# Second products of a feed-forward turned round: weights stationary, 512 tokens moving

## The chip, the cores and the metric

The kernel runs on one core of a Trainium2 chip. The metric is the device time of one execution in microseconds. The engines are TensorE (PE; PEld is its weight load), VectorE (DVE), ScalarE (ACT), GpSimd (POOL) and SyncE (SP); the last two mainly start DMAs here.

## The reference

A block of a network: the input plus a state-space convolution plus a feed-forward, both of the layer-normed input.

```python
# x: 1 x 2048 x 576, state size 128, hidden size 4608
xn = (x - mean(x)) / sqrt(var(x) + 1e-5)
dt = exp(log_dt); A = A_re + 1j*A_im
K  = real(einsum("dn,dnl,dn->dl", C, exp(dt*A*l), dt*B))     # response, 2048 long
y  = irfft(rfft(pad(xn)) * rfft(pad(K)))[:2048] + xn * Dskip
h  = silu(xn @ w1)
out = x + y + h @ w2
```

## The kernel before

The feed-forward is the main work. The 2048 tokens are taken in two halves; the hidden size is cut into 9 chunks of 4 tiles of 128; and a block is a half, a chunk and 512 tokens (`b` 0 or 1), so there are 36 blocks. All its matmuls are made in the fast fp32r format, and each operand is split into a high and a low part (`h`, `l`), of which three products are summed.

A block has eight steps. `u0` to `u3` (`up`, L343 to L345) each make one hidden tile: 14 matmuls with 128x128 of w1 stationary and 512 tokens moving into a PSUM bank `ph`; ScalarE then makes the silu `gf` (L351) and the high part `gh` (L352), VectorE the low part `gl` (L354). `d0` to `d3` (`down`, L369) each take 128 tokens: `gh` or `gl` of 128 tokens is stationary, and 288 columns of `w2h` or `w2l` move, 12 matmuls for each half of the 576 columns, into a bank `po`. VectorE adds the bank to `acc` (L373), which begins as x. That is 96 matmuls of 288 columns in a block. `u0` of the next block stands ahead of `d0`, and `u1` to `u3` stand behind `d3`. The banks `ph` come from a round of two (`ps1`), `po` from another of two (`ps2`), and every third `po` from a fifth bank (`ps3`).

Beside this, a generator `side` makes the convolution: layernorm and transposes (`pt`, L134), the parameters, the first transform of the inputs (`spread`: `xr` loaded, split into `sp` by L166 and L167, multiplied into `pu` by L171 and L172, copied by L173, sent out as `d1u` by POOL), the response (`kgen`, 36 steps; each odd step makes `kp`, L708, 32-column tiles, then `z`, L723, two row tiles of 64, copies it to `stage` by L731 and sends it to `d1k`), the spectral stage (`pf`, L804; `pb`, L848), and the last transform (`py`, L963) with the sum. `weave` runs both generators: the side yields the share of the main steps at which it goes on. From this a scheduler that simulates the engines fixes the order of the instructions on each engine; `high_priority` and `behind` (not ahead of a named instruction) bend it. At run time each engine takes its list in order.

```python
        while at is not None and at * steps <= i + 1:
            at = next(side, None)
```

The sums of the first half go to DRAM (`dr0`), and are loaded back at the end to get their convolution added.

Of the kernel before, what the change touches and what calls it, by code (L numbers as in the profile page):

```python
# [43 lines left out]
def kernel(  # L44
# [24 lines left out]
    NCH = NFT // FT  # L69

# [15 lines left out]
    dr0 = dram.tile([8 * P, D], F32, name="dr0")  # L86
# [17 lines left out]
    accp = ctx.enter_context(tc.tile_pool(name="accp", bufs=4))  # L104
# [3 lines left out]
    ps1 = ctx.enter_context(tc.tile_pool(name="ps1", bufs=2, space=PSUM))  # L108
    ps2 = ctx.enter_context(tc.tile_pool(name="ps2", bufs=2, space=PSUM))
# [4 lines left out]
    def banks_of():  # L114

        n = 0
        while True:
            n += 1
            pool, tag = (ps3, "ps3") if ps3 and n % 3 == 0 else (ps2, "ps2")
            yield pool.tile([P, 512], F32, tag=tag, name="po")  # L120

    spare = banks_of()
# [32 lines left out]
    def spread(up):  # L155

        s1 = up.tile([P, 2, P], F32R, name="s1", bufs=1)
        nc.gpsimd.dma_start(s1, cs1)
        for j in range(NJ):
            src = up.tile([P, D], F32, tag="xr", name="xr")  # L160
            nc.sync.dma_start(src, dxn[:, j])
            for m in range(2):
                lo, hi = slice(64 * m, 64 * m + 64), slice(64 - 64 * m, 128 - 64 * m)
                u1 = up.tile([P, D], F32, tag="u1", name="u1")
                sp = up.tile([P, D], F32R, tag="sp", name="sp")
                nc.scalar.copy(sp[lo, :], src[lo, :])  # L166
                nc.vector.tensor_sub(sp[hi, :], src[lo, :], sp[lo, :])  # L167
                for h in range(2):
                    hs = slice(h * HD, (h + 1) * HD)
                    pu = pss.tile([P, 512], F32, tag="pss", name="pu")  # L170
                    nc.tensor.matmul(pu[:, :HD], s1[:, 0, :], sp[:, hs], start=True, stop=False)  # L171
                    nc.tensor.matmul(pu[:, :HD], s1[:, 1, :], sp[:, hs], start=False, stop=True)  # L172
                    nc.scalar.copy(u1[:, hs], pu[:, :HD])  # L173
                nc.gpsimd.dma_start(  # L174
                    d1u.rearrange("(p m j) d -> m j p d", m=2, j=NJ)[m, j], u1)
                yield j
# [44 lines left out]
    def phase0(p0, js, idle=None):  # L221

        xs = load_x(js[0], accp, "acc", (nc.sync, nc.scalar) if js[0] < 2 else (nc.sync,))
        acc.update(zip(js, xs))
# [42 lines left out]
    def ffn():  # L267
# [42 lines left out]
        def load_w2(half, c, t):  # L310

            first = half == 0 and c == 0
            last = half == 1 and c == NCH - 1
            r2 = (pa if first and t > 1 else yp if last and t > 1 else wp).tile([P, D], F32, tag="w2r", name="w2r", bufs=2 if t > 1 and (first or last) else 3)
            landed = nc.sync.dma_start(r2, w2v[:, c * FT + t, :]).ins
            if t < 2:
                pins["load"] = landed
            R2[half, c, t] = r2

        def split_w2(half, c, t):  # L320
            first = half == 0 and c == 0
            r2 = R2.pop((half, c, t))
            h2 = wp.tile([P, D], F32R, tag="w2h", name="w2h", bufs=FT + 1)
            l2 = wp.tile([P, D], F32R, tag="w2l", name="w2l", bufs=FT + 1)
            with behind(pins["xt_s"] if first else pins["gh"]):
                pins["w2h"] = nc.scalar.copy(h2, r2).ins
            with behind(pins["w1l"] if first else None):
# [3 lines left out]
            W2[half, c, t] = h2, l2  # L331

        def up(blk, t, a=0, e=512, after=None):
# [4 lines left out]
            pool, tag = (None, "") if e == 256 and t > 1 else (ps1, "ps1")  # L338
            ph = (pool.tile([P, 512], F32, tag=tag, name="ph") if pool else next(spare))[:, a:e]
# [16 lines left out]
        def down(blk, jj):  # L356
# [3 lines left out]
            if half == 1 and c == NCH - 1:  # L360
                if jj % 2 == 0:
                    add_conv(j, (acc[j], acc[j + 1]))
            for h in range(2):
                hs = slice(h * HD, (h + 1) * HD)
                po = next(spare)
                n = 0
                for t in range(FT):
                    for g, w in ((0, 0), (0, 1), (1, 0)):
                        pins["pe"] = nc.tensor.matmul(po[:, :HD], G[blk, t][g][:, js], W2[half, c, t][w][:, hs],  # L369
# [4 lines left out]
            if half == 0 and c == NCH - 1:  # L374
                rows = slice(j * P, (j + 1) * P)
                nc.sync.dma_start(dr0[rows, :], acc[j])
                if j % 2:
                    acc[7 + j], acc[8 + j] = load_x(7 + j, accp, "acc", (nc.sync,))
# [32 lines left out]
        yield 0  # L411

# [7 lines left out]

        for i, blk in enumerate(blocks):
            half, c, b = blk
            later = i + 1 < len(blocks)
            new = (half, c + 1) if c + 1 < NCH else (half + 1, 0)
            more = new[0] < 2
            if half == 0 and c == NCH - 1:
# [7 lines left out]
                (1, "d3"): [(split_w2, 1), (load_w2, 3), (split_w2, 2)],  # L434
                (1, "u2"): [(split_w2, 3)],
            }
            if new == (1, NCH - 1):
# [5 lines left out]
                    (1, "d3"): [(split_w2, 1), (split_w2, 2)],  # L443
                    (1, "u2"): [(split_w2, 3)],
                }
            for step in ("u0", "d0", "d1", "d2", "d3", "u1", "u2", "u3"):
                k = int(step[1])
                if step[0] == "d":
                    down(blk, k)
                    yield 3.0  # L450
                elif later:
                    up(blocks[i + 1], k)
                    yield 3.0
                for f, t in after.get((b, step), ()) if more else ():
                    f(*new, t)
                if half == 0 and c == NCH - 1:
# [25 lines left out]
    def natural(nat, par):  # L482
# [32 lines left out]
        lrT = nat.tile([P, D], F32, tag="lrT", name="lrT")  # L515
# [639 lines left out]
```

## Time and profile before

| | |
|---|---|
| median of 3 runs | 1099.55 us (1099.28 to 1099.86) |
| profiled execution | 1099.23 us, of which the span of instructions is 1097.4 |
| granted TensorE clock | 1.00 of full speed |
| busy | PE 1090.0, PEld 963.2, DVE 888.0, ACT 658.9, POOL 136.6 us |
| stages (by the side's work) | start to 40 us, inputs and response to about 650, spectral 673 to 960, last transform to the end |

Times are microseconds from the start of the span. In rows that group instructions, the number behind the bar is busy time, then the mean in ns, then the idle time of the engine before them and what ended it. Matmuls overlap in the pipeline, so the mean duration of one is longer than its share of time; the chain of waits gives the share, since it lists how much later the next piece began.

### The profile page before, as it was taken

Reading aid. Unit: us, or ns where it says so; the run is one execution under the profiler, and the core shown is the slowest. Engines: PE = TensorE matmul, PEld = TensorE weight load, DVE = VectorE, ACT = ScalarE, POOL = GpSimd, SP = SyncE. Lnnn points to the kernel's source line nnn. Section 1 sums busy time; section 2 is a strip of 40 time slices with the busy share of each in tenths; the row PEclk is TensorE's granted clock in tenths of the full one; section 3 lists DMA queues with packets and bytes.
Section 4 is the critical chain, followed back from the end, with each engine's and each line's share of the span. In section 5 each row is a group of like instructions: output and inputs, shape, how many; then the busy total and the mean of one; then the engine's idle time right before and its main releaser. Section 6 shows DMA issues by size and latency. Waiting matters only on the chain.

```text
span 1097.4 us, 23933 instructions
## 1 busy us (share of the span) xinstructions
PE 1090.0 (99%) x9807; PEld 963.2 (88%) x9807; DVE 888.0 (81%) x1431; ACT 658.9 (60%) x1030; POOL 136.6 (12%) x241
## 2 busy tenths in 40 slices
PE   9999999999999999999999999999999999999998
PEld 7989998999889898999899988888888888898886
DVE  7799899999999999989999945886777777753443
ACT  4575457666776676677766744675676656552220
POOL 1101000000000000010000024223232312000111
PEclk9999999999999999999999999999999999999999
DMA  9845522524343525264755147356555545326953
GB/s 257 219 124 156 147 62 62 121 70 112 95 99 108 108 73 126 80 138 141 201 151 120 65 95 240 120 163 179 176 184 147 159 132 175 120 95 167 240 162 88
DMA packets 174142, 150.23 MB, mean 137 GB/s; under 512 B 112288, under 2 KB 143792, under 8 KB 173904
## 3 DMA queue, kind: packets, MB, share of 16 engines
q1 hardware_dynamic: 156544, 93.77, 33.4%
q0 software_dynamic: 16736, 54.07, 15.7%
q8 instruction: 77, 1.26, 0.5%
q10 hardware_dynamic: 752, 0.85, 0.3%
q14 instruction: 33, 0.27, 0.1%
HBM read 104.13 MB, written 44.61 MB: 136 GB/s over the span
## 4 chain that ended last, share of the span: by engine, by line
PE 98%; DVE 1%; DMA 0%; issue 0%; POOL 0%; ACTq 0%; DVEq 0%; ACT 0%
PE po L369 42%; PE ph L343 36%; PE kp L708 3%; PE pf L804 3%; PE ph L345 3%; PE ph L344 3%; PE pb L848 2%; PE z L723 2%; PE pu L171 1%; PE py L963 1%; PE pu L172 1%; PE pt L134 0%; DMA acc<-in_A_u_dram 0%; DVE w1l L305 0%; DVE st L203 0%; PE ptk L502 0%
## 5 line engine op out<-in xcount | busy, mean ns | idle before, releaser
L369 PE MATMUL po<-w2h,gh 128*128 128x288 f32 x1152 | 338.4, 296 | 0.0
L369 PE MATMUL po<-w2l,gh 128*128 128x288 f32 x1152 | 337.4, 295 | 0.0
L369 PE MATMUL po<-w2h,gl 128*128 128x288 f32 x1152 | 335.9, 296 | 0.0
L369 PEld LDWEIGHTS po<-w2h,gh 128*128 128x128 f32 x1152 | 215.5, 188 | 13.6 <-issue 5.3
L369 PEld LDWEIGHTS po<-w2l,gh 128*128 128x128 f32 x1152 | 215.6, 188 | 6.9 <-issue 1.1
L369 PEld LDWEIGHTS po<-w2h,gl 128*128 128x128 f32 x1152 | 214.9, 188 | 1.6 <-issue 0.2
L373 DVE TENSOR_TENSOR acc<-po,acc 128x288 f32<-128x288 f32 x288 | 125.9, 450 | 101.5 <-PE po L369 100.2
L351 ACT ACTIVATE gf<-ph 128x512 f32<-128x512 f32 (+1 forms) x146 | 85.7, 588 | 178.9 <-PE ph L345 164.0
L343 PE MATMUL ph<-xl,w1h 128*128 128x512 f32 (+1 forms) x584 | 159.1, 387 | 0.0
L343 PE MATMUL ph<-xh,w1h 128*128 128x512 f32 (+1 forms) x584 | 158.7, 388 | 0.0
L343 PE MATMUL ph<-xh,w1l 128*128 128x512 f32 (+1 forms) x584 | 158.7, 386 | 0.0
L354 DVE TENSOR_TENSOR gl<-gf,gh 128x512 fp32r<-128x512 f32 (+1 forms) x148 | 98.1, 669 | 47.8 <-ACT gh L352 47.1
L343 PEld LDWEIGHTS ph<-xl,w1h 128*128 128x128 f32 x584 | 107.1, 188 | 21.3 <-issue 0.7
L343 PEld LDWEIGHTS ph<-xh,w1l 128*128 128x128 f32 x584 | 107.0, 188 | 20.2
L343 PEld LDWEIGHTS ph<-xh,w1h 128*128 128x128 f32 x584 | 104.0, 188 | 18.1 <-issue 0.8
L352 ACT CAST gh<-gf 128x512 fp32r<-128x512 f32 (+1 forms) x148 | 89.1, 610 | 39.3 <-PE po L369 36.5
L174 POOL DMA_DIRECT2D d1u<-u x32 | 17.4, 543 | 462.3 <-ACT u L173 460.4
L667 ACT ACTIVATE c<-th 128x1040 f32<-128x1040 f32 x36 | 38.7, 1075 | 45.9 <-DVE th L666 45.9
L665 ACT ACTIVATE c<-th,magic 128x1040 f32<-128x1040 f32 x36 | 42.1, 1168 | 26.1 <-DVE C L688 23.2
L305 DVE TENSOR_TENSOR w1l<-w1r,w1h 128x640 fp32r<-128x640 f32 x72 | 56.8, 816 | 0.1
L345 PE MATMUL ph<-x,w1l 128*128 128x512 f32 (+1 forms) x146 | 56.7, 389 | 0.0
L344 PE MATMUL ph<-x,w1h 128*128 128x512 f32 (+1 forms) x146 | 56.5, 388 | 0.0
(195 smaller groups left out, 1725.9 us busy)
## 6 DMA issues: line engine op xcount, KB each, us to landing
w2r<-in_B_w_dram SPq DMA_DIRECT2D x72, 288.0 KB, 4.3
w1r<-in_B_w_dram SPq DMA_DIRECT2D x35, 512.0 KB, 3.9
d1u<-u POOLq DMA_DIRECT2D x32, 288.0 KB, 2.9
d1k<-stage SPq DMA_DIRECT2D x36, 256.0 KB, 4.8
u<-d1u POOLq DMA_DIRECT2D x16, 576.0 KB, 5.6
kw<-d1k POOLq DMA_DIRECT2D x16, 576.0 KB, 4.7
d<-yo POOLq DMA_DIRECT2D x32, 288.0 KB, 3.0
ys<-d SPq DMA_DIRECT2D x32, 288.0 KB, 8.5
```

The source lines that it names most:

```text
L305: pins["w1l"] = nc.vector.tensor_sub(l1, src, h1).ins
L343: nc.tensor.matmul(ph, w[:, kt, :], v[:, kt, a:e], start=n + kt == 0, stop=False)
L344: nc.tensor.matmul(ph, h1[:, 4, :], x4[:, a:e], start=False, stop=False)
L345: pins["pe"] = nc.tensor.matmul(ph, l1[:, 4, :], x4[:, a:e], start=False, stop=True).ins
L351: nc.scalar.activation(gf, ph, AF.Silu)
L352: pins["gh"] = nc.scalar.copy(gh, gf).ins
L354: pins["gl"] = nc.vector.tensor_sub(gl, gf, gh).ins
L369: pins["pe"] = nc.tensor.matmul(po[:, :HD], G[blk, t][g][:, js], W2[half, c, t][w][:, hs], start=n == 0, stop=n == 3 * FT - 1).ins
L373: nc.vector.tensor_add(acc[j][:, hs], po[:, :HD], acc[j][:, hs])
L665: nc.scalar.activation(c65, th, AF.Identity, bias=magic)
L667: nc.scalar.activation(c65, th, AF.Abs)
L708: mm = nc.tensor.matmul(dst, t[:, ch, :32], t[:, ch, 32:], start=begins and n == 0, stop=True, tile_position=(0, 32 * q), skip_group_check ...
```

## The change

For the first half's nine chunks and the second half's first five (`SW = 5`; 28 of 36 blocks) `down` is replaced by `across`. There 128 columns of w2 are stationary and 512 tokens move, so a bank holds 128 of the 576 output columns for all 512 tokens. Banks `k` = 0 to 3 take 12 matmuls each; the last 64 columns take 8, since the high and the low part of w2 stand side by side in one 128-wide operand (in a bank's two halves of rows, added later). That is 56 matmuls of 512 columns in a block and one step more, `d4`. In the first block banks 0 and 1 are made in two pieces of 256 tokens. VectorE copies (chunk 0) or adds the five banks to transposed sums of 128 x 5 x 512. `w2h` and `w2l` are now one tile `w2s`, with a copy by ScalarE of 64 columns per tile (L447 and its like).

After the last chunk of each such run, `turn_out` transposes the sums on VectorE in squares of 32 and SP writes them to DRAM in pieces of 128 bytes (18 DMAs for each 512 tokens); POOL adds x in DRAM (`add_x`); for the second half's last four chunks SP loads them back (`load_acc`), and `down` goes on as before.

The banks of `ph` and `po` now come from one round of four, every fifth from `ps3` while it exists. `spread` is gone: the inputs' first transform is made in `kgen`'s odd steps by two matmuls in full fp32 of 512 columns on the same two row tiles as `z`, and the copies of `z` and `pu` out of PSUM come one step later. The marks that pace the side go from 0.13, 0.597, 0.876 to 0.13, 0.61, 0.88, with a slower stretch around the change of halves; `mm` has one buffer instead of two.

```diff
+        def one(blk, k, a, e):
+            half, c, b = blk
+            at = sums[half, b][:, k, a:e]
+            po = bank("po")[:, a:e]
+            ks = slice(k * P, min(D, (k + 1) * P))
+            terms = [(W2[half, c, t][:, (D + 64) * (1 - w):][:, ks], G[blk, t][g][:, a:e]) for t in range(FT) for g, w in ((0, 0), (0, 1), (1, 0))]
+            if k == NKT:
+                terms = [(W2[half, c, t][:, k * P:k * P + P], G[blk, t][g][:, a:e]) for t in range(FT) for g in range(2)]
+            for n, (w, g) in enumerate(terms):
+                pins["pe"] = nc.tensor.matmul(po, w, g, start=n == 0, stop=n == len(terms) - 1).ins
+            with tc.high_priority():
+                if c == 0:
+                    nc.vector.tensor_copy(at, po)
+                else:
+                    nc.vector.tensor_add(at, po, at)
...
+    def bank(name):
+        ring.append(name)
+        pool, tag = (ps3, "ps3") if ps3 and len(ring) % 5 == 0 else (ps1, "ps1")
+        return pool.tile([P, 512], F32, tag=tag, name=name)
...
+        def turn_out(half, b, k):
+            at = sums[half, b][:, k]
...
+            nc.vector.transpose(at[:32 * n], at[:32 * n])
+            for a in range(n):
+                d0 = k * P + 32 * a
+                nc.sync.dma_start(rows[:, :, d0:d0 + 32], at[32 * a:32 * a + 32].rearrange("i (c k) -> i c k", k=32))
...
+        moves = {
+            (last + 1, "u2"): [(add_x, (0, 0))],
+            (last + 2, "u2"): [(add_x, (0, 1))],
+            (turned, "u1"): [(add_x, (1, 0))],
+            (turned, "u3"): [(load_acc, (0,))],
+            (turned + 1, "u1"): [(add_x, (1, 1))],
+            (turned + 1, "u3"): [(load_acc, (1,))],
+        }
...
+        for t in range(FT):
+            hl, r2 = R2.pop((0, 0, t))
+            with behind(pins["gh"] if "gh" in pins else None):
+                nc.scalar.copy(hl[:, D:D + 64], r2[:, NKT * P:])
...
+                src, v = us.pop(), i // 2
+                pu = [pss.tile([P, 512], F32, tag="pss", name="pu") for _ in range(2)]
+                for m in (1, 0):
+                    rows = slice(64 * m, 64 * m + 64)
+                    with tc.high_priority(), behind(first):
+                        nc.tensor.matmul(pu[m], s1[rows], src[rows], start=True, stop=True, tile_position=(64 * m, 0))
+                load_in(v + 1)
+                later = copies(i, v, z, pu)
...
-        marks = (0.13, 0.597, 0.876)
+        marks = (0.13, 0.61, 0.88)
```

The order on ScalarE at the start, before: first the casts of w1, then the silu of the first hidden tile.

```order
L303 CAST w1h<-w1r 128x640 x2
L351 ACTIVATE gf<-ph 128x256
L352 CAST gh<-gf 128x256
L351 ACTIVATE gf<-ph 128x256
L352 CAST gh<-gf 128x256
```

The same place after the change.

```order
L287 CAST w1h<-w1r 128x640 x2
L447 CAST w2s<-w2r 128x64
L338 ACTIVATE gf<-ph 128x256
L339 CAST gh<-gf 128x256
L338 ACTIVATE gf<-ph 128x256
L339 CAST gh<-gf 128x256
```

A copy that reads the first load of w2 now stands ahead of the first silu.

TensorE at the end of the first block's hidden tiles, before (`ph_608` is the last tile's second half of tokens, `po_674` to `po_716` are banks of `down`, `pt` transposes of the normed input; numbers tell tiles of one name apart).

```order
L369 MATMUL po_674<-w2h_282,gl_472 128x288
L369 MATMUL po_688<-w2h_282,gl_472 128x288
L369 MATMUL po_702<-w2h_282,gl_472 128x288
L343 MATMUL ph_608<-xh_0_165,w1h_258 128x256 x4
L343 MATMUL ph_608<-xl_0_166,w1h_258 128x256 x4
L343 MATMUL ph_608<-xh_0_165,w1l_259 128x256 x4
L344 MATMUL ph_608<-x4_0_167,w1h_258 128x256
L345 MATMUL ph_608<-x4_0_167,w1l_259 128x256
L134 MATMUL pt_310<-ident_69,xn_303 128x128 x4
L369 MATMUL po_716<-w2h_270,gh_408 128x288
```

And after (`ph_603` is the last tile, `po_670` a piece of 256 tokens, `po_767` a bank of 512).

```order
L332 MATMUL ph_603<-x4_0_163,w1l_255 128x256
L377 MATMUL po_670<-gh_404,w2s_266 128x256 x2
L377 MATMUL po_670<-gl_405,w2s_266 128x256
L377 MATMUL po_670<-gh_425,w2s_269 128x256 x2
L377 MATMUL po_670<-gl_426,w2s_269 128x256
L377 MATMUL po_670<-gh_446,w2s_272 128x256 x2
L377 MATMUL po_670<-gl_447,w2s_272 128x256
L377 MATMUL po_670<-gh_467,w2s_275 128x256 x2
L377 MATMUL po_670<-gl_468,w2s_275 128x256
L377 MATMUL po_767<-gh_404,w2s_266 128x512 x2
L377 MATMUL po_767<-gl_405,w2s_266 128x512
L377 MATMUL po_767<-gh_425,w2s_269 128x512 x2
```

Before, single products of `down` stand between the hidden tiles' matmuls, three of them open at a time; now the second products all follow the last hidden tile, and nine products further on the transposes `pt_302`, `pt_309`, `pt_343` and `pt_350` come within one bank's work.

TensorE in an odd step of the response, before: the last two `z` of eight, and one pair of the inputs' transform behind them.

```order
L723 MATMUL z_1987<-f1_108,kt_1984 128x128
L723 MATMUL z_1986<-f1_108,kt_1984 128x128
L171 MATMUL pu_2104<-sp_2101,s1_2096 128x288
L172 MATMUL pu_2104<-sp_2101,s1_2096 128x288
L369 MATMUL po_2169<-w2h_1540,gh_1751 128x288
```

And after (`z_1789` and `pu_1799` use rows 64 to 127 of the array, `z_1788` and `pu_1798` rows 0 to 63).

```order
L820 MATMUL z_1789<-f1_1299,kt_1786 128x128
L820 MATMUL z_1788<-f1_1299,kt_1786 128x128
L828 MATMUL pu_1799<-xr_1316,s1_1314 128x512
L820 MATMUL z_1789<-f1_1299,kt_1786 128x128
L820 MATMUL z_1788<-f1_1299,kt_1786 128x128
L828 MATMUL pu_1798<-xr_1316,s1_1314 128x512
L820 MATMUL z_1789<-f1_1299,kt_1786 128x128
L820 MATMUL z_1788<-f1_1299,kt_1786 128x128
L377 MATMUL po_1965<-gh_1833,w2s_1512 128x512 x2
```

The two 512-column matmuls stand between the eight `z`, with two more `z` between them.

More of the change, by code (lines that the diff above doesn't have):

```diff
@@ L85 @@
     dxn = dram.tile([P, NJ, D], F32, name="dxn")
-    dr0 = dram.tile([8 * P, D], F32, name="dr0")
+    drs = [dram.tile([8 * P, D], F32, name=f"dr{half}") for half in range(2)]
     dexp = dram.tile([P, D, 3], F32, name="dexp")
@@ L153, in behind, with pieces @@
         return tc.issue_after(ins) if ins is not None else nullcontext()
[L155 to L176, printed above, removed]
+    def pieces(v):
+        at = 512 * v
+        while at < 512 * (v + 1):
+            j, c = divmod(at, D)
+            n = min(D - c, 512 * (v + 1) - at)
+            yield j, c, n, at - 512 * v
+            at += n
     def load_x(j, pool, tag, engines):
@@ L373, in down, with across @@
                     nc.vector.tensor_add(acc[j][:, hs], po[:, :HD], acc[j][:, hs])
[L374 to L378, printed above, removed]
+        def across(blk, k):
+            half, c, b = blk
+            if c == 0 and k == 0:
+                sums[half, b] = accp.tile([P, 5, 512], F32, tag="acc", name="acc")
+            for a, e in ((0, 256), (256, 512)) if half + c + b == 0 and k < 2 else ((0, 512),):
+                one(blk, k, a, e)
@@ L419, in ffn, with turns @@
             yield 3.0
+        sums = {}
+        last, turned = 2 * NCH - 1, 2 * (NCH + SW) - 1
+        def turns(half, c, b, k):
+            return c == (SW if half else NCH) - 1
+        moves = {
[6 more added lines that the diff above has]
+        }
         for i, blk in enumerate(blocks):
@@ L423, in ffn @@
             later = i + 1 < len(blocks)
+            ends = half == 1 and c >= SW
             new = (half, c + 1) if c + 1 < NCH else (half + 1, 0)
@@ L455, in ffn @@
                     f(*new, t)
+                for f, args in moves.get((i, step), ()):
+                    f(*args)
                 if half == 0 and c == NCH - 1:
@@ L514, in natural @@
         v.tensor_mul(aim, aim, dtb)
[L515 removed]
+        lrT = phiT
         turned(are, lrT)
```

254 lines of the change are left out of this document (146 added, 108 removed).

## The prediction

> **What bounds the kernel now.** The page comes first: busy time and the chain that ended last.
>
> ```profile
> span 1097.4 us, 23933 instructions
> ...
> PE 1090.0 (99%) x9807; PEld 963.2 (88%) x9807; DVE 888.0 (81%) x1431; ACT 658.9 (60%) x1030; POOL 136.6 (12%) x241
> ...
> PE 98%; DVE 1%; DMA 0%; issue 0%; POOL 0%; ACTq 0%; DVEq 0%; ACT 0%
> ```
>
> TensorE works 1090.0 of 1097.4 us and is 98% of the chain. So the kernel takes as long as TensorE's list of matmuls, plus the few places where the list stands still. A change gains only by a shorter list or by fewer standstills; work taken off another engine gains nothing by itself. The chain in order of time, in a quiet stretch, gives the prices of the list:
>
> ```profile
> 643.61 1.09 PE z L723 x16
> ...
> 646.29 2.72 PE ph L343 x12
> ...
> 649.46 3.18 PE po L369 x24
> 652.64 2.74 PE ph L343 x12
> ```
>
> A 512-column product (`ph`) costs 2.72/12 = 0.2267 to 2.74/12 = 0.2283 us, a 288-column product (`po`) 3.18/24 = 0.1325 us. By columns alone 512 should cost 1.78 times 288; it costs 1.72 times, since each product also has a fixed part: from the two prices, (0.2283 − 0.1325)/224 = 0.428 ns a column and 9 ns fixed. Standstills that the profile can see on TensorE ahead of the end are few. This is the view of waits on TensorE for the first 40 us:
>
> ```profile
> PE pt L134 <- DVE xn L212: 1.1, 2, 0.9
> ```
>
> The windows view shows whether a loaded VectorE already holds TensorE back in the long middle (columns: stretch, length, busy us of PE, PEld, DVE, ACT, POOL):
>
> ```profile
> 110.00:560.00 450.00, 450.00 (x4552) 406.35 (x4551) 430.92 (x649) 304.31 (x459) 18.83 (x34) 1.00 0.43 111
> ```
>
> VectorE is busy 96% there, and TensorE still never stands still.
>
> **Second products turned round.** In 28 of the 36 blocks (18 of the first half, 10 of the second) 96 products of 288 columns become 56 of 512. At 0.1325 the block cost 12.72 us. At 0.2283 it costs 56 × 0.2283 = 12.78; at 0.2267, 12.70; at 0.2300 (the 640 us row below) 12.88.
>
> ```profile
> 639.96 1.38 PE ph L343 x6
> ```
>
> I take 0.2285, inside that spread: 12.80, so +0.08 a block and **+2.2 us** over 28 (−0.6 to +4.5). The saving in number of products is eaten by columns: 28,672 a block instead of 27,648. Block 0 does two of its five banks in pieces of 256 columns, 48 products for 24:
>
> ```profile
> 14.05 0.64 PE L343 MATMUL po<-xh,w1h 128*128 128x256 f32 x4
> 14.53 0.64 PE L343 MATMUL po<-xl,w1h 128*128 128x256 f32 x4
> ```
>
> Four take 0.48 us from start to start, 0.12 each: 48 × 0.12 = 5.76 against 24 × 0.2285 = 5.48, **+0.3**.
>
> The Trainium skill, page "TensorE: Matmul & The Clock Gate", section "Back-to-back issue gap", puts a warm product at N/2.4 + 2.5 ns, that is 122.5 ns for 288 and 215.8 ns for 512 (an estimate from that page: 11.76 us against 12.08 a block, +9 us in all). The trace disagrees with it on both sizes, 132.5 and 227 to 228 ns, so its fixed part is too small for these products and the measured prices stand.
>
> **Evictions.** Eight additions of 288 columns a block become five of 512.
>
> ```profile
> L373 DVE TENSOR_TENSOR acc<-po,acc 128x288 f32<-128x288 f32 x288 | 125.9, 450 | 101.5 <-PE po L369 100.2
> L354 DVE TENSOR_TENSOR gl<-gf,gh 128x512 fp32r<-128x512 f32 x140 | 94.9, 684 | 47.4 <-ACT gh L352 46.7
> L167 DVE TENSOR_TENSOR sp<-xr,sp 64x576 fp32r<-64x576 f32 x32 | 24.1, 753 | 1.0
> L260 DVE STREAM_TRANSPOSE tr<-xj 128x576 f32<-128x576 f32 x8 | 5.9, 760 | 0.0
> ```
>
> 8 × 0.450 = 3.60 us before; 5 × 0.684 = 3.42 after, by the nearest 512-column row. VectorE also loses 24.1 us of `sp` and gains 20 transposes of about 0.7 us. All of that lies beside products: a bank now fills in 12 × 0.2285 = 2.74 us instead of 1.59 and the round has four banks, so an eviction may be late by several us. Cost 0. If that cover were gone, each block would wait for one VectorE instruction of some 0.7 us, 20 us in all.
>
> **The inputs' first transform.** Before, 128 products of 288 columns in 64 pairs:
>
> ```profile
> 326.31 0.13 PE pu L171
> 326.44 0.13 PE pu L172
> 326.57 0.13 PE pu L171
> 326.70 0.13 PE pu L172
> ```
>
> 128 × 0.1325 = 16.96 us, besides interruptions that `z` pays anyway. After, each odd step of the response puts two full-precision products of 512 columns between the eight `z`, on row tiles of 64. What one costs is seen in the spectral stage, where eight such tiles run side by side:
>
> ```profile
> 729.82 1.09 PE L804 MATMUL pf<-kw,m 64*32 64x512 f32 x16
> 730.70 1.06 PE L804 MATMUL pf<-u,m 64*32 64x512 f32 x16
> ```
>
> One batch after the other starts 0.88 us later. Do the two halves run at the same time though the program has other work between them? `kp` answers: L708's loops alternate C and S on each column tile, but the timeline has eight C first (four tiles, two passes each) and then eight S:
>
> ```profile
> 304.70 0.34 PE L708 MATMUL kp<-C 128*32 128x64 f32 x8
> 304.84 0.32 PE L708 MATMUL kp<-S 128*32 128x64 f32 x8
> 304.95 0.32 PE L708 MATMUL kp<-C 128*32 128x64 f32 x7
> ```
>
> So an instruction that waits for its tile does not hold back a later one on a free tile. Then the lower rows can do their `z` and `pu` while the upper ones do theirs, and an odd step grows by one 0.88: 18 × 0.88 = 15.84 us, **−1.1** against 16.96. Strictly in order it would grow by 1.76: 31.7 us, +14.7 (first rival). The nearest row of the same kind is `kp`, so I take −1.1.
>
> ACT's copies of `z` and `u` wait for the next even step; nothing queued behind them is late by more than one step, and the first spectral product comes at 672.8, some 28 us after the end of the `z` run at 643.61:
>
> ```profile
> L804 PE MATMUL pf<-kw,m x512: 216/415/614, 672.8 to 959.3; 64*32 64x512 f32 x22, 64*32 64x384 f32 x22, 64*32 64x192 f32 x22, 64*32 64x320 f32 x22
> ```
>
> The loads of `xr` on SP and the `d1u` pieces on POOL have whole steps of slack. Cost 0.
>
> **The start.** Here the list changes most, and here VectorE and ACT really end waits:
>
> ```profile
> 10.61 2.42 SPq L315 DMA_DIRECT2D w2r<-in_B_w_dram  x4
> w2r<-in_B_w_dram SPq DMA_DIRECT2D x72, 288.0 KB, 4.3
> 14.28 0.38 ACT L351 ACTIVATE gf<-ph 128x256 f32<-128x256 f32 x1
> 14.69 0.41 ACT L352 CAST gh<-gf 128x256 fp32r<-128x256 f32 x1
> 15.82 0.75 DVE L354 TENSOR_TENSOR gl<-gf,gh 128x256 fp32r<-128x256 f32 x2
> 16.50 1.07 DVE L212 TENSOR_SCALAR xn<-acc,mv,sd 128x576 f32<-128x576 f32 x2
> 17.14 1.15 PE L134 MATMUL pt<-ident,xn 128*128 128x128 f32 x8 [0.20 <-DVE xn L212]
> ```
>
> The new order has ACT's 64-column copy of the first `w2r` ahead of the first silu. That load is issued at 10.6 and lands 4.3 to 4.5 later, about 15.0; with the copy (at most 0.27, as the 128-column row of L813 below) the silu starts near 15.3, 1.05 late. `gl` and, behind it in VectorE's order, `xn` follow, and TensorE's `pt` with 0.2 already waited: about +0.85.
>
> ```profile
> L813 ACT COPY ka<-pf 128x128 f32<-128x128 f32 x4 | 1.1, 266 | 1.3 <-PE pf L804 1.3
> ```
>
> The second part: before, 288-column `po` products of single tiles stand between the `up` products of block 0's second half, and fill the time in which silu, cast and subtraction (0.38 + 0.41 + 0.42) make the rest. Now all four `up` come first; `po_670` (12 × 0.12 = 1.4 us) covers little, and `po_767` needs the second halves of all four tiles, three of which by my placement leave ACT and VectorE only after 29 us. The transposes `pt_343` and `pt_350`, now earlier in the list, need banks that ACT's `xh` and VectorE's `xl` have yet to empty. Placing the new order by hand with these durations, I get 4.3 us of standstill by 41 us where the waits above show 1.1: **+3.3** (an estimate; 0.5 if only the copy's part shows in half, 6 if the bank waits add up).
>
> **Turning out and reloading.** After blocks 26 and 27 the sums go out in 18 writes of 128-byte pieces, POOL adds x in DRAM, and SP loads the whole back for blocks 28 and 29. Nearest rows, and POOL's worst neighbour:
>
> ```profile
> d1k<-stage SPq DMA_DIRECT2D x36, 256.0 KB, 4.8
> r<-dr SPq DMA_DIRECT2D x4, 576.0 KB, 10.4
> POOL mm L779 <- PE pb L848: 82.4, 13, 20.9
> ```
>
> Chain: 4.8 for the last write, at most 10.4 for the additions, 10.4 for the load: 25.6 us. From block 26's last second product to block 28's first lie eight `up` and one block of second products: 8 × 14 × 0.2285 + 12.8 = 38.4 us, plus spectral runs. Slack 13 us or more: cost 0. In blocks 16 and 17 the same writes only free a buffer, needed 38 us later. On SP the loads of the next `w1r` and `w2r` stand behind the reload, on POOL `mm` behind the additions; both are issued more than a block ahead of use.
>
> **The sum.** +2.2 + 0.3 − 1.1 + 3.3 = +4.7. The profiled execution took 1099.23 (span 1097.4 and 1.8 around it), the median is 0.3 above it: 1103.9 on the one, **1104.2** on the other, say 1104. The terms' own ends give 1099 to 1109. Differences within 0.2%, 2.2 us, are what a measurement of this kernel can't tell from no change.
>
> **Rivals.** *Row tiles in program order*: `pu` and the `z` behind it queue up, an odd step grows by 1.76 us, 18 times: 1104.2 + 15.8 = 1120. Against it speak the `kp` rows; for it, that no row shows a long instruction at the head of a tile's queue with several behind it. Chance 0.12. The Trainium skill's page named above, section "The mechanism", says that matmuls start and end strictly in program order, only weight loads being pulled ahead; by that rule this rival would be the forecast. The eight C before eight S at 304.70 speak against it as far as this trace goes.
>
> *Faster*: the fixed part shrinks in the turned products. All 1,568 of them share the price, so 1 ns is 1.57 us. `ph` rows already spread over 3.3 ns; the new runs use each `gh` twice in a row and rarely end on a wait. From 0.2241 down (2.2 + 4.7 = 6.9 us, over 1.57, 4.4 ns below 0.2285) the kernel is measurably faster; at 0.2225 it takes 1094.8. For it: 512 columns alone take 512 × 0.428 = 219 ns. Against it: no run shown is below 0.2267. Chance 0.13.
>
> *The reload is late*: if POOL waits its 20.9 us ahead of the additions, the chain is 46.5 us against 38 to 43, so block 28 stands still for 4 to 8 us, and block 29 may do the same: 1108 to 1112, more if it repeats. It decides once POOL's wait is over 13 us. For: 13 waits of that kind, with a mean of 6.3. Against: the additions stand ahead of the next `mm` there. Chance 0.06.
>
> **How the numbers follow.** Forecast 0.69, own range 1099 to 1109; I give 0.20 of it to the last few us, where low ends of two terms meet and the result lies within 0.2%. Faster 0.13 comes from the second rival alone; slower is 0.49 + 0.12 + 0.06 = 0.67. The range 1096.5 to 1115 leaves out the first rival and half of the second, 0.19.
>
> **What would show it.** Right: runs of the new second products at 2.74 us for 12; VectorE and ACT waits on TensorE of about 4 us by 41 us; `z` runs with `pu` inside of about 2.0 us (1.09 + 0.88). Wrong: such runs of 2.9 us or more (in order), products under 0.2241 or over 0.2315, a gap of over 2 us on TensorE between 780 and 900 us, or waits in the response stage on VectorE's new evictions.

## The result and the profile after

The changed kernel takes 1108.38 us (median of 6 runs, 1106.05 to 1111.52) against 1099.41 (6 runs, 1099.01 to 1099.86): ratio 1.0082, 95% interval 1.0065 to 1.0099. It is slower by some 9 us, nearly twice the 4.7 of the forecast's sum, and inside the range (the terms' own ends had given 1099 to 1109). The profiled execution was its quickest, 1106.05, at a granted clock of 1.00; the run of 1106.49 was at 1.00 too, and the other four, 1108.1 to 1111.5, at 0.996 to 0.998. The median therefore lies 2.3 us above what the profile shows.

The page of the kernel after, busy time:

```profile
span 1104.3 us, 21613 instructions
...
PE 1090.7 (99%) x8655; PEld 895.0 (81%) x8655; DVE 881.3 (80%) x1341; ACT 653.5 (59%) x1042; POOL 158.2 (14%) x257
```

TensorE's busy time has hardly moved (1090.0 before), with 1,152 instructions fewer. The span is longer by 6.9, and the waits of over 0.15 us on TensorE add up to 9.6 us where they were 2.9. So the list of matmuls is about as long as it was, and the time went into standstills. The windows view of the kernel after says where (columns as above: stretch, length, busy us of PE, PEld, DVE, ACT, POOL):

```profile
110.00:560.00 450.00, 446.90 (x3766) 364.98 (x3765) 410.96 (x584) 285.55 (x430) 29.49 (x38) 1.00 0.42 107
...
660.00:960.00 300.00, 297.76 (x2254) 241.40 (x2253) 222.62 (x329) 188.01 (x322) 93.88 (x162) 1.00 0.67 189
```

In 110 to 560 VectorE is less busy than before (411 us for 431), and yet TensorE, which never stood still there, now does so for 3.1 us; in 660 to 960 for 2.2. The timeline of the kernel after, TensorE, has each of the larger waits with what ended it:

```profile
28.20 0.70 PE L377 MATMUL po<-gh,w2s 128*128 128x512 f32 x2 [0.61 <-DVE sd L192]
33.78 0.63 PE L133 MATMUL pt<-ident,xn 128*128 128x128 f32 x4 [0.98 <-DVE xl L135]
35.09 1.19 PE L330 MATMUL ph<-xh,w1h 128*128 128x512 f32 x4 [0.46 <-ACT xh L134]
126.37 0.50 PE L377 MATMUL po<-gh,w2s 128*128 128x512 f32 x1 [2.34 <-DVE acc L382]
548.71 0.96 PE L330 MATMUL ph<-xh,w1h 128*128 128x512 f32 x3 [0.77 <-DVE acc L382]
848.05 0.37 PE L942 MATMUL pb<-yh,mm 128*128 128x288 f32 x1 [0.96 <-DMA mm<-in_cm_dram]
891.94 0.99 PE L898 MATMUL pf<-u,m 64*32 64x64 f32 x32 [1.27 <-DMA u<-d1u]
```

Three kinds stand here: the start (28 to 36 us), banks that VectorE empties late (126, 549), and loads of the spectral stage that come late (848, 892). For the second kind, VectorE's timeline of the kernel after, ahead of the wait at 126:

```profile
116.72 0.19 DVE L192 TENSOR_SCALAR sd<-mv 128x2 f32<-128x2 f32 x1
...
120.73 0.58 DVE L197 TENSOR_SCALAR xj<-xj,mv,sd 128x576 f32<-128x576 f32 x1 [0.54 <-POOL sd L193]
...
124.31 1.43 DVE L244 STREAM_TRANSPOSE tr<-xj 128x576 f32<-128x576 f32 x2
125.66 1.25 DVE L382 TENSOR_TENSOR acc<-po,acc 128x512 f32<-128x512 f32 x2
```

The eviction at 125.66 is that of block 3's first bank, which TensorE had filled near 115.7 (12 products from 112.99 on). VectorE works without a pause worth naming on what stands ahead of it in its list. Of that, the normalisation of one token tile (`sd`, 0.54 us of waiting for POOL's answer, `xj`, its bias `mb`, two `tr`) makes 2.9 us, more than TensorE's wait of 2.34. In those ten us the other banks of the round fill up. For the third kind, POOL's timeline of the kernel after (it issues DMAs, and waits in order):

```profile
835.65 3.60 POOL L400 DMA_DIRECT2D dr<-in_A_u_dram  x4 [7.87 <-DMA dr<-acc]
837.95 1.89 POOL L873 DMA_DIRECT2D mm<-in_cm_dram  x1
...
877.16 3.62 POOL L400 DMA_DIRECT2D dr<-in_A_u_dram  x4 [15.42 <-DMA w2r<-in_B_w_dram]
...
884.93 0.74 POOL L860 DMA_DIRECT2D u<-d1u  x1 [1.39 <-DMA dr<-in_A_u_dram]
```

The additions of x (L400) wait for the last write of turned-out sums, 7.9 and 15.4 us (the second wait is put down to a load of `w2r` that stands behind the last writes in SP's queue and landed 0.6 us after them), and the loads of `mm` and `u` that the spectral stage wants stand behind the additions.

### The profile page after: what moved, and what is told of

It is laid out like the page before. It is cut to its first block, busy times and chain, and to the rows that moved or that the text cites. A ratio compares the mean times of both kernels' runs of the same rounds, so it can differ in the third digit from the quotient of the medians.

```text
span 1104.3 us, 21613 instructions
## 1 busy us (share of the span) xinstructions
PE 1090.7 (99%) x8655; PEld 895.0 (81%) x8655; DVE 881.3 (80%) x1341; ACT 653.5 (59%) x1042; POOL 158.2 (14%) x257
## 4 chain that ended last, share of the span: by engine, by line
PE 70%; DVE 14%; DMA 8%; issue 2%; SPq 2%; ACT 2%; POOL 1%; ACTq 0%; DVEq 0%; POOLq 0%
PE ph L330 26%; PE po L377 22%; PE po L355 8%; PE kp L805 3%; PE pf L898 2%; PE ph L332 2%; PE ph L331 2%; PE pb L942 2%; PE z L820 1%; DMA w2r<-in_B_w_dram 1%; DMA w1r<-in_B_w_dram 1%; DVE acc L382 1%; PE pu L828 1%; DMA mm<-in_cm_dram 1%; DVE th L760 1%
## 5 line engine op out<-in xcount | busy, mean ns | idle before, releaser
L377 PE MATMUL po<-gh,w2s 128*128 128x512 f32 (+1 forms) x1024 | 321.1, 388 | 2.9 <-DVE acc L382 2.3
L377 PEld LDWEIGHTS po<-gh,w2s 128*128 128x128 f32 x1024 | 190.5, 188 | 45.8 <-issue 3.0
L377 PE MATMUL po<-gl,w2s 128*128 128x512 f32 (+1 forms) x568 | 217.9, 390 | 0.0
L377 PEld LDWEIGHTS po<-gl,w2s 128*128 128x128 f32 x568 | 106.6, 188 | 22.8 <-DVE gl L341 0.4
L382 DVE TENSOR_TENSOR acc<-po,acc 128x512 f32<-128x512 f32 x120 | 80.7, 684 | 29.8 <-PE po L377 29.5
L355 PE MATMUL po<-w2s,gh 128*128 128x288 f32 x512 | 103.2, 296 | 0.0
L355 PEld LDWEIGHTS po<-w2s,gh 128*128 128x128 f32 x512 | 82.0, 188 | 5.1 <-issue 3.8
L355 PE MATMUL po<-w2s,gl 128*128 128x288 f32 x256 | 74.7, 295 | 0.0
L310 ACT CAST w2s<-w2r 128x576 fp32r<-128x576 f32 x72 | 48.2, 674 | 29.7 <-PE po L377 18.6
L784 DVE TENSOR_TENSOR S<-th,C 128x1024 f32<-128x1024 f32 x36 | 44.0, 1221 | 21.4 <-ACT th L762 21.3
```

What stands on the lines that cost most here:

```text
L377: pins["pe"] = nc.tensor.matmul(po, w, g, start=n == 0, stop=n == len(terms) - 1).ins
L382: nc.vector.tensor_add(at, po, at)
L784: nc.vector.tensor_mul(ov3, t[:, :, 0:64].rearrange("n d (x y) -> n d x y", y=32), mv3)
```

## The experiments

Two theories stood at first. Mine: the list is as long as before, and the time is lost in these three kinds of waits, each with its own cause in the order of a queue. The rival: the products themselves, or the pairing of the change's parts, cost the time, and curing waits only moves them. Line numbers of the changed kernel shift by a few in the experiments. All ratios are against the kernel before.

**late_add: POOL's additions behind the loads.** The steps move a little within their blocks, and each addition is put behind one load of `mm` or `u`.

```diff
-            (turned, "u1"): [(add_x, (1, 0))],
-            (turned, "u3"): [(load_acc, (0,))],
-            (turned + 1, "u1"): [(add_x, (1, 1))],
+            (turned, "u0"): [(add_x, (1, 0))],
+            (turned, "d2"): [(load_acc, (0,))],
+            (turned + 1, "d0"): [(add_x, (1, 1))],
...
+                    with behind(pins["held" if args[1] else "first"] if f is add_x and args[0] else None):
+                        f(*args)
```

> The changed kernel with one thing moved: POOL's additions of x for the second half's reload stand one load of `mm` (block 26) and one load of `u` (block 27) later in POOL's list, so that these loads no longer stand behind an instruction that waits for the turned-out writes. Theory (the order on POOL does it): TensorE's waits at `pb` for `mm` (1.0 us) and at `pf` for `u` (1.3 us) go, no new wait of over 0.5 us between 840 and 910 us; the median falls from 1108.4 by 2 to 4 us, since this part also changes from run to run, and the runs lie closer together. Rival (the writes in 128-byte pieces and the additions themselves crowd the DMA queues, whatever their order): the waits stay or move to another load, and the time stays within 1 us.

1106.61 us (1105.50 to 1108.72), ratio 1.0067 (1.0054 to 1.0079). The gain of 1.8 us is a little less than the expected 2 to 4, and the two intervals overlap, so the time alone decides nothing. But after 654 us TensorE waits nowhere in the profile, and late_tile below, which keeps this edit, repeats that: the cause of these two waits is shown. The rival was right in part. Behind the additions the load of `mm` took 10.0 us from issue to landing, ahead of them 3.2; so its place in POOL's order and a slower transfer behind the additions both made it late. The profiled execution had the wait on VectorE at its worst, and behind it something that no row of before has. Timeline of late_add, TensorE:

```profile
129.07 0.79 PE L377 MATMUL po<-gh,w2s 128*128 128x512 f32 x1 [3.75 <-DVE acc L382]
129.66 0.63 PE L377 MATMUL po<-gl,w2s 128*128 128x512 f32 x1
130.09 0.63 PE L377 MATMUL po<-gh,w2s 128*128 128x512 f32 x1
130.51 0.63 PE L377 MATMUL po<-gl,w2s 128*128 128x512 f32 x1
...
132.65 1.86 PE L330 MATMUL ph<-xh,w1h 128*128 128x512 f32 x4
134.34 1.10 PE L330 MATMUL ph<-xl,w1h 128*128 128x512 f32 x4
```

Start to start these products take 0.425 us, not 0.227, for some 11 products; the windows view gives a granted clock of 0.57 there. So here the wait cost its own length and then about 11 × 0.2 = 2.2 us of half speed.

```profile
130.00:135.00 5.00, 5.00 (x14) 3.86 (x13) 5.00 (x9) 1.64 (x4) 0.00 (x0) 0.57 1.00 194
```

**late_copy: the small copies of w2 behind the silu.** ScalarE's four 64-column copies of chunk 0 move behind all first halves of the hidden tiles.

```diff
         for t in range(FT):
-            hl, r2 = R2.pop((0, 0, t))
-            with behind(pins["gh"] if "gh" in pins else None):
-                nc.scalar.copy(hl[:, D:D + 64], r2[:, NKT * P:])
```

> The changed kernel with ScalarE's 64-column copies of w2 for the first chunk put behind the silu of block 0's first token half instead of ahead of the first silu. By the prediction's first part of the start (0.85 us) the wait of `pt` for `xn` at 17 us falls from 0.4 to 0.2 or less and the kernel gains 0.5 to 0.9 us. By the trace of the changed kernel, where the load lands at 14.5 and the wait at 17 us is only 0.18 longer than before, the gain is 0.2 us or less, and the waits at 28 and 33 us stay.

1109.89 us (1108.33 to 1113.95), ratio 1.0100 (1.0082 to 1.0117): no gain. The wait at 17 us fell from 0.38 to 0.20, the others at the start stayed. ScalarE's timeline of the kernel after tells why:

```profile
14.54 0.24 ACT L447 CAST w2s<-w2r 128x64 fp32r<-128x64 f32 x1 [0.62 <-DMA w2r<-in_B_w_dram]
14.69 0.38 ACT L338 ACTIVATE gf<-ph 128x256 f32<-128x256 f32 x1
```

The load landed at 14.5, not at 15.0, and the silu begins 0.15 us behind the copy's start, at 14.69 for 14.28 before. Of these 0.4 us late, moving the copy took 0.2 off TensorE's wait.

**two_rounds: two banks for `ph` and two for `po`.** This is nearly the layout of before. There, however, the third and fourth hidden tiles of the first 256 tokens took their banks from `po`'s round; here every `ph` takes one of its own two.

```diff
-    ps1 = ctx.enter_context(tc.tile_pool(name="ps1", bufs=4, space=PSUM))
+    ps1 = ctx.enter_context(tc.tile_pool(name="ps1", bufs=2, space=PSUM))
+    ps2 = ctx.enter_context(tc.tile_pool(name="ps2", bufs=2, space=PSUM))
```

> The changed kernel with the banks of before: a round of two for `ph`, a round of two for `po`, every third `po` from the fifth bank while it exists. Theory (four banks in one round give an eviction some 8 us of lag, and the wait of 2.3 us at 126 us is VectorE's list, which has the eviction 10 us after its bank was full): with two banks for five evictions a block TensorE waits in many blocks of the response stage; 10 us slower or more. Rival (the common round itself makes `po` wait for a bank of `ph` and makes the waits at 126 and 549 us): those go, and the kernel is 2 to 4 us faster.

1109.07 us (1107.58 to 1110.01), ratio 1.0083 (1.0069 to 1.0097), the same as with one round. The waits at 28 to 35, 126, 549, 848 and 892 us are gone, and others came: 1.4 us at 15.8 (the third hidden tile, for want of the bank just named) and at 52.4 on ScalarE's `gf`, 2.0 at 916 on the cast of `w1h`. My expectation of 10 us or more was wrong, and the rival was right on the waits and wrong on the gain: without the common round other waits come. The waits on `mm` and `u` went although the additions had not moved: the load of `mm` again took 10.0 us, but landed 0.5 us before TensorE came to it. So the additions make these loads late, and the rest of the order decides whether TensorE notices. The waits in this profile add up to 7.7 us against 9.6, yet its span is 1.5 us longer: of these 3.4 us, `z` with `pu` took 2.1 over the whole response, and the rest was not traced.

**pu_only and pu_round: the inputs' first transform alone.** In the kernel before, `spread` is replaced by the two matmuls in the odd steps, with the copies a step later (the same code as in the change); pu_round adds the one round of four.

```diff
+                sined = nc.scalar.activation(c65, c65, AF.Sin, scale=-TWO_PI, bias=halfpi).ins
+                if i % 2 == 0:
+                    with behind(sined):
+                        next(later, None)
```

> The kernel before with one part of the change alone: the inputs' first transform in the response's odd steps (two full-precision products of 512 columns between the eight `z`, copies a step later, four banks for it and no fifth bank for `po` in the response); second products as before. By the prediction the list of TensorE shrinks by 1.1 us: 1098.3. By the trace of the changed kernel, where a run of `z` with `pu` takes 2.05 us instead of 1.09 and the resumption behind it is paid as before, the list grows by 0.4 us: 1099.5 to 1100, more only if `po` with two banks waits for VectorE. If the two row tiles ran one after the other, it would be 1112 or more.

> The kernel pu_only (the kernel before with the inputs' first transform in the response's runs, 1111.9) with one round of four banks for `ph` and `po`, every fifth from the fifth bank while it exists, as the change has it; second products as before. Theory (pu_only's 12 us are waits for a bank: `ph` has a round of two that ScalarE's silu frees late, behind the copies of `z` and `pu`, and `po` has lost its third): they fall to 3 us or less, 1100 to 1103. Rival (ScalarE's and VectorE's lists are late for the work itself, the silu and the evictions, whatever the banks): 1108 or more.

pu_only: 1111.85 us (1111.56 to 1113.94), ratio 1.0114 (1.0100 to 1.0128). Both forecasts were wrong by 12 us or more. The 1112 named for row tiles that run one after the other is met in number only: `z` with `pu` takes 2.05 us in most runs of this profile too and 2.10 on average, not 2.85. TensorE now waits on ScalarE; the waits of pu_only, and ScalarE's timeline ahead of one of them, at 578:

```profile
PE ph L329 <- ACT gf L337: 5.6, 5, 2.6
```

```profile
572.65 1.08 ACT L689 ACTIVATE c<-th 128x1040 f32<-128x1040 f32 x1 [0.77 <-DVE th L688]
573.76 1.08 ACT L690 ACTIVATE th<-th 128x1040 f32<-128x1040 f32 x1
574.75 1.15 ACT L691 ACTIVATE c<-c,halfpi 128x1040 f32<-128x1040 f32 x1
575.80 1.12 ACT L661 COPY stage<-z 128x512 f32<-128x512 f32 x2
576.80 1.08 ACT L671 COPY u<-pu 128x512 f32<-128x512 f32 x2
577.75 0.63 ACT L337 ACTIVATE gf<-ph 128x512 f32<-128x512 f32 x1
```

Three activations of the response and now four copies come in one piece ahead of a silu, 5.1 us, and two `ph` banks are not enough to bridge it. These waits are 5.6 of the 12.8 us by which the span grew; other waits make 2.7, `z` with `pu` 1.1, and the rest was not traced. pu_round, with four: 1112.42 us (1110.74 to 1113.97), ratio 1.0121 (1.0106 to 1.0137). The waits on `gf` are gone, and the time is the same; the 1100 to 1103 of its theory fell, and the rival's 1108 or more came out. Other waits came in their place, 2.3 us between 28 and 35 us and two larger ones behind VectorE; timeline of pu_round, TensorE:

```profile
68.88 0.40 PE L351 MATMUL po<-w2h,gl 128*128 128x288 f32 x1 [2.00 <-DVE gl L336]
...
76.12 0.40 PE L351 MATMUL po<-w2h,gh 128*128 128x288 f32 x1 [3.26 <-DVE acc L355]
```

It shows a second thing. In pu_round the second products are not turned, and the waits of 0.64, 0.96 and 0.46 us at 28.5, 32.2 and 34.9 us are there much as in the kernel after; in two_rounds the products are turned, and no wait over 0.1 us stands between 16 and 52 us. So the start's waits from 28 us on come with the common round, not with the turned products.

**turn_only: the turned products and the round, with the old `spread`.** The edit puts `spread` and its copies back into the changed kernel.

> The changed kernel with its other part undone: the inputs' first transform made as before (`sp`, 128 products of 288 columns beside the response), sent out in halves of 288 columns, `eb` with one buffer; turned second products, round of four and turn-out as in the change. Theory (the turned products shorten TensorE's list by 1.6 us, the transform in the response's runs lengthens it by 0.4, and the loss is waits at the start, for evictions and for POOL): 1106 to 1109, about the changed kernel's time, with the same waits at 28 to 35, near 126 and from 845 to 895 us. Rival (the change needs the 24 us that VectorE saves by losing `sp`): more eviction waits in the response, 1112 or more.

1119.30 us (1117.99 to 1122.08), ratio 1.0182 (1.0168 to 1.0196), 11 us slower than with both parts. The theory's 1106 to 1109 fell. The rival, too, holds in the total only: the windows view of turn_only has VectorE near its load of before again, but TensorE's standstill in that stretch is 2.9 us, no more than the 3.1 of the kernel after.

```profile
110.00:560.00 450.00, 447.15 (x3815) 368.22 (x3814) 427.66 (x608) 303.91 (x480) 38.14 (x65) 1.00 0.43 107
```

What is large is one wait in the spectral stage. Three timelines of turn_only, TensorE, VectorE and POOL:

```profile
894.76 0.85 PE L368 MATMUL po<-w2s,gh 128*128 128x288 f32 x2 [7.94 <-DVE acc L372]
```

```profile
893.52 0.82 DVE L859 SCALAR_TENSOR_TENSOR kw<-kw,cwt 128x576 f32<-128x576 f32 x1 [9.89 <-DMA kw<-d1k]
894.25 0.45 DVE L372 TENSOR_TENSOR acc<-po,acc 128x288 f32<-128x288 f32 x1
```

```profile
877.52 3.64 POOL L413 DMA_DIRECT2D dr<-in_A_u_dram  x4 [11.76 <-DMA w2r<-in_B_w_dram]
...
880.95 2.10 POOL L842 DMA_DIRECT2D kw<-d1k  x1
```

This is the third kind again and dearer: the additions hold back POOL's loads of `kw`, VectorE stands still for 9.9 us at the first use of `kw`, and an eviction that is ready stands behind that. So the order on POOL, and not VectorE's load, took the largest piece. That is read from the rows; moving the additions in this kernel was not tried. The rest (2.3 us at 574 behind ScalarE's `gf`, 1.3 at 959, a clock of 0.994 to 0.997 in the runs) has no single cause. One part at a time costs some 12.5 us (pu_only) and 20 us (turn_only), both together 9: the costs do not add. The rows fit the reading that each part moves waits of the other; it was not shown further.

**late_tile: two normalisations moved away.** From late_add, the last two token tiles of the second half are normalised 18.5 main steps later, so that no normalisation stands ahead of an eviction near 126 us.

```diff
-                        for at, todo in ((0.0, nt), (0.0, tiles), (1.15, tiles), (1.44, tiles), (5, nt), (7.5, tiles), (8.5, tiles), (11.4, tiles), (11.9, tiles), (14, nt), (19.5, tiles), (23, nt), (28.5, nt)):
+                        for at, todo in ((0.0, nt), (0.0, tiles), (1.15, tiles), (1.44, tiles), (5, nt), (7.5, tiles), (8.5, tiles), (11.4, tiles), (11.9, tiles), (14, nt), (23, nt), (28.5, nt), (38, tiles)):
```

> The kernel late_add (the changed kernel with POOL's additions moved) with one thing more: the normalisation and turning of the last two token tiles (`xj`, `tr`) is emitted 18 main steps later, so that VectorE's list has the additions of block 3's banks ahead of it. Theory (VectorE's list, which has block 3's first eviction behind two transposes that wait for POOL, makes the wait at 126 to 129 us): no wait over 1 us between 100 and 150 us, 2.3 to 3.8 us less waiting, no half-speed products behind it; median 1103 to 1104.5 and all clocks 1.000. Rival (VectorE has too much work there and the wait only moves to another bank): a wait of 2 us or more elsewhere before 200 us, and 1106 to 1107 as late_add.

1102.88 us (1101.96 to 1104.52), ratio 1.0031 (1.0020 to 1.0043), 3.7 us less than late_add. The wait near 126 is gone, and with it the half speed: all six runs have a clock of 0.999 or 1.00. The cause of the large wait of the second kind is shown. The small one at 549 stays (0.68 us, at 547). Late in the kernel the loads are in time as in late_add, though TensorE now comes to them earlier than in the kernel after; the waits of late_tile on TensorE from 640 to 960 us are this one line:

```profile
PE kp L810 <- DVE C L790: 0.2, 1, 0.2
```

**marks_only: the new marks in the kernel before.**

```diff
-        marks = (0.13, 0.597, 0.876)
+        marks = (0.13, 0.61, 0.88)
```

> The kernel before with the change's two later marks alone (0.61 and 0.88 for 0.597 and 0.876): every operation is the same, only the side's work from the response on is emitted a little later, so the lists of all engines are laid out anew from there. Theory (the loss is not in the operations but in a few places where a list laid out from simulated times misfits the chip, and the order of before happens to have almost none): TensorE waits 3 to 8 us in two to four places after 110 us, and the median is 1101 to 1108. Rival (the waits come from what the change adds, its evictions, turn-out and start): TensorE waits less than 2.5 us in all, and the time is within 1 us of 1099.4.

1099.40 us (1099.10 to 1099.73), ratio 1.0000 (0.9991 to 1.0009). This re-laid order loses nothing, so the theory fell; the waits come from what the change adds.

**between: first halves of second products among the hidden tiles.** From late_tile, block 0's banks 0 to 3 are all made in pieces of 256 tokens, the first pieces between the hidden tiles' second halves.

```diff
             up(blocks[0], t, 256, 512)
+            one(blocks[0], t, 0, 256)
             yield 3.0
```

> late_tile, and block 0's banks 0 to 3 are each made in two pieces of 256 tokens, the first pieces standing between the hidden tiles of the second 256 tokens, as single products of the second kind stood before the change. Theory (the waits at 28 to 36 us come from the round of four being handed to four hidden tiles in a row, with nothing of the second kind between them): the waits between 25 and 37 us, 2.0 us in late_tile, fall below 1.0; the list grows by 0.3 to 0.5 us for the further pieces; median 1101.0 to 1102.5. Rival (the chain of silu, cast and subtraction, or the copies behind the transposes, is late by itself): the waits stay at about 2 us and move by a few us at most, and the median is 1102.9 to 1103.5.

1100.88 us (11 runs, 1099.69 to 1102.86), ratio 1.0014 (1.0005 to 1.0023). Between 25 and 37 us one wait is left; TensorE's timeline of between:

```profile
29.21 0.52 PE L379 MATMUL po<-gl,w2s 128*128 128x256 f32 x3
29.57 0.64 PE L330 MATMUL ph<-xh,w1h 128*128 128x256 f32 x4
...
36.98 1.20 PE L330 MATMUL ph<-xh,w1h 128*128 128x512 f32 x4 [0.51 <-ACT xh L134]
```

The waits there fell from 2.0 to 0.5 us, and the median by 2.0: a bank of the round that is filled by a product whose operands are ready is what the start lacked. (One new wait, 1.0 us at 852 on ScalarE, came with it.) With the three cures the kernel is 7.5 us quicker than the changed one and within 0.2% of the kernel before, not below it. No version that ran beats the kernel before.

## Why the prediction was right, and where it was not

The sign was right, the time lay in the range, and the main step held: the list hardly changes, and standstills decide. But the rise was nearly twice the forecast, and most of it lies in two terms that the prediction put at 0, evictions and turn-out. That the sum came as near as it did is in part luck, since errors of both signs cancel. Here are its terms in the profiled execution, over all matmul records from one start to the next (for the prices, products with a wait or a change of kind behind them are left out; the start's term is all the time to 41 us that is not the price of a product, 16.4 against 13.4 us; a restart is what the product behind a wait takes longer than others):

| term | forecast | measured |
|---|---|---|
| turned products | +2.2 | 1,568 × 227.63 ns against 2,688 × 132.47 ns: +0.8 |
| block 0's pieces | +0.3 | 48 × 0.119 − 24 × 0.2276: +0.3 |
| first products `ph` | none | 1,960 × (227.5 − 228.9) ns: −2.7 |
| inputs' transform | −1.1 | 18 × 0.96 = 17.3 against 16.96: +0.3 |
| start (to 41 us) | +3.3 | +3.0 |
| evictions | 0 | 2.34 + 0.77 and two restarts: +3.4 |
| turn-out, reload | 0 | 0.96 + 1.27 and two restarts: +2.5 |
| median over profile | 0.3 | 2.3 |

The terms of the profile add up to +7.6; the last matmul starts 7.4 later than before.

- **Products.** The step "I take 0.2285" was mis-sized. Undisturbed whole blocks run at 0.2266, the low end of the prices quoted from the shorter runs of before. Chain of the kernel after:

```profile
231.52 12.69 PE po L377 x56
...
304.05 2.72 PE ph L330 x12
```

  12.69 us stand against 12.72 of before. The `ph` products got cheaper too, which fits that they now follow products of their own size (that was not tried by itself); the prediction gave each kind its own fixed price and missed this. The second rival's direction was right and its bound (0.2241) was not reached.
- **Inputs' transform.** The step "an odd step grows by one 0.88" was a little small. Chain of the kernel after, one odd step, and the stretch behind it:

```profile
203.40 0.65 PE z L820 x8
204.05 0.21 PE pu L828
204.26 0.11 PE z L820
204.37 0.64 PE pu L828 x3
205.01 0.44 PE z L820 x5
205.45 0.66 PE po L377 x2
```

  The run takes 2.05 us where `z` alone took 1.09: +0.96, not +0.88, and not the +1.76 of the first rival. The row tiles do work side by side past each other's waits, as `kp` had said; the strict order of the Trainium skill's page "TensorE: Matmul & The Clock Gate", section "The mechanism", does not fit these rows.
- **Start.** The size was right, the working half wrong, so its fit is luck in part: of the +3.0 only 1.7 are waits in the profile (2.75 us for 1.1), and "about +0.85" for the copy is about 0.2 by the wait that it moved (late_copy), and most of the waits belong to the common round (pu_round, two_rounds, between).
- **Evictions at 0.** This step failed. "An eviction may be late by several us" was sized for one VectorE instruction, but what stood ahead in VectorE's order was ten us of work, 116 to 126, more than the round of banks covers. It shows where the prediction said it would if the prediction was wrong, although the time stayed in the range: "waits in the response stage on VectorE's new evictions".
- **Turn-out and reload at 0.** The reload itself came in time, as worked out. "On POOL `mm` behind the additions; both are issued more than a block ahead of use" failed: `mm` now has one buffer and `u` waits behind additions that wait up to 15.4 us, so the order on POOL, and not the chain to the sums, was the price. In the kernel after the load of `mm` was issued 9 us before TensorE wanted it and took 10.0. The third rival's own mechanism, the sums late for block 28, appeared in no run.
- **Median.** "0.3 above" was taken over from a kernel without long waits. Where TensorE waits for some us, some runs pay for it again at half speed: four of the changed kernel's six runs had a clock of 0.996 to 0.998.

What stays open: late_tile and between still have 4.7 and 3.9 us of standstill against 1.7 before (all without the 1.3 us at the very start that every version has), and which part of the last 1.4 us is owed to which of them was not tried.

## What to carry to other kernels

When one engine is busy 99% of the time, count what a change adds to its list, and then look at every in-order queue that the change lengthens: what stands ahead of the small step that frees a bank or starts a load, and for what does that wait? Slack counted in one engine's mean load (VectorE 91%) says nothing about one eviction behind ten us of other work. And parts of a change that each lose on their own may carry one another: test them alone and together.

## What the runs showed of the hardware

After a wait of 3.75 us TensorE ran some 11 products of 512 columns at 0.425 us each, and in late_copy's profile the products behind a wait of 1.70 us did so too; timeline of late_copy, TensorE (four products from 894.58 to 896.28):

```profile
892.95 0.99 PE L897 MATMUL pf<-u,m 64*32 64x64 f32 x32 [1.70 <-DMA u<-d1u]
...
894.58 1.91 PE L330 MATMUL ph<-xl,w1h 128*128 128x512 f32 x4
896.28 1.74 PE L330 MATMUL ph<-xh,w1l 128*128 128x512 f32 x4
```

In late_copy small 64x32 tiles stand around the wait, and what part they have in it is not shown. The wait of 2.34 us in the profile of the kernel after was followed by no half speed, nor was that of 3.26 us in pu_round's, whose granted clock stays at 1.00 there. The Trainium skill, page "TensorE: Matmul & The Clock Gate", section "What's actually happening", says that TensorE falls to half its clock after an idle window of about 3.4 us, and that the windows run freely. That the same kind of wait is punished in one execution and not in another fits the free running; if the wait alone did it, the 1.70 us of late_copy are less than the page's window. Each wait of these rows also made the next product about 0.1 us longer: the one behind the wait at 126.37 took 0.34 us to the next start, not 0.227. So many short waits cost more than their sum.
